# Folding mirrored rows before stage one of a Fourier mixing and maxout kernel

## The chip, the cores and the metric

The kernel runs on one core of a Trainium2 chip. A core has five engines with queues of their own: TensorE (PE in the profile; its weight loads are PEld) multiplies matrices, VectorE (DVE) and ScalarE (ACT) work on elements, GpSimd (POOL) copies, adds and starts indirect DMAs, and SyncE (SP) starts most DMAs. The metric is the device time of one execution in microseconds.

## The reference

For 8 batches of 3072 tokens by 256 features, the input goes through a Fourier transform over tokens and one over features; the real part is kept. Each of the 24576 tokens then goes through a maxout layer:

```python
X = np.fft.fft(x, axis=1); X = np.fft.fft(X, axis=2); y = X.real
h = np.maximum(np.maximum(y @ w1, y @ w2), y @ w3)      # 256 -> 768
out = h @ w_out                                         # 768 -> 256
```

The input is real. So the result of a feature pair d and 64 - d (in the kernel's layout of four groups of 64 features) can be got from a few real sums, and the token k and its mirror image 3072 - k share most of the work.

## The kernel before

**Stage one** (method `s` of `Mix`, pieces s0 to s6). Tokens are split as 24 x 128. A batch lies on 96 partitions, four groups of 24: partition (g, a) holds feature group g of token row a, with 128 tokens bb and 64 features dl along the free axis. TensorE takes, for a feature d of 33, the 96x128 rows as weights and a table of 96 columns as the moving operand. Each feature needs two matmuls into the same PSUM columns: one (L496) with the rows as they are and the table m24f, one (L498) with the *mirrored* rows (feature 64 - d of the mirrored token) and m24r. Pieces s0 to s5 do five features each; s6 does features 0 (52 columns), 32 (48) and 1 (96). The result z is evicted by ScalarE (L503).

**The rows for it** (`turn_chunk`, `reverse`). A batch is loaded in four chunks of 32 token columns, fp32, into a pool of four tiles xs (L107; the chunk's one extra row by L119). GpSimd casts each chunk to bf16 and to the order feature by token: two casts for the rows as they are (L155, `v[:, 0:33]`) and two for the mirrored ones (L158, `v[:, 33:66]`, read backwards within the partition). The bf16 tile x0 is in a pool of two. Batch 0 is loaded as bf16 and laid out by ScalarE and VectorE during the set-up.

**Stage two** (pieces k0 to k5, `end`). TensorE multiplies z with tables (L522, L524); ScalarE evicts to t, whose halves tE and tO are the even and odd parts of a batch (two buffers).

**The layer.** A batch is 18 *units*: 3 blocks of 512 columns by 6 chunks of 128 hidden features. `unit_plus` (L542, L543) makes two PSUM banks pse2 and pse3 from te and to; ScalarE takes the relu of the first (L556, tile stmp), VectorE the maximum with the second (L557, tile hp). `finish`, one unit later, subtracts through gD into the same banks (`unit_minus`, L550) and again makes relu and maximum (tile hm): that is the mirrored half of the tokens. pse2 and pse3 have two banks each, so `unit_plus` of a unit waits until hm of the unit but one before is read out. The second product (L567) is spread between the units as a queue of small steps (`l2_some`); per 128 tokens VectorE makes other (L594) and ot (L617), GpSimd adds even (L597) and scatters half of ot by an indirect DMA (L620), and SP stores the other half (L630). ot is in a pool of six.

**Order.** Every engine runs its queue in the order in which the program emits it. A table `plan` says which work is emitted behind which unit; `at(b, unit, fn)` counts units from the start of batch b and runs over into the next batch. While batch b is multiplied, the pieces of batch b + 1 are emitted one per unit from `begin[b]` on, the casts of batch b + 2 behind units 6 to 21, and the loads of batch b + 3 behind units 18, 19, 20 and 22 (that is 0, 1, 2 and 4 of the next batch; 6 after batch 0). SP's queue holds loads and stores together.

## Time and profile before

| | us |
|---|---|
| median of 3 runs | 413.23 |
| lowest, highest | 412.5, 413.6 |
| profiled execution | 412.64 |
| its span | 410.9 |
| VectorE, hp and hm (L557), 288 of | 0.69 each |
| VectorE, ot (L617) and other (L594), 92 of each | 0.68 and 0.48 each |
| GpSimd, casts (L155, L158) of 96x512 to 96x561 | 1.05 to 1.16 each |
| GpSimd, even (L597) and scatter (L620), 92 of each | 0.72 and 1.12 each |

How to read it: the profile gives each engine's busy time and its share of the span; a chain of waits, followed back from the last instruction; the queue of every engine as a timeline (start, duration, engine, line, output<-inputs, partitions x elements; in brackets the idle time before and what ended it); and waits by engine. Busy is not the same as bound: matmuls overlap, so a matmul's cost is the distance between starts. The 1.7 us between the span and the execution's time lie around the program.

### The profile page before, as it was taken

What the parts mean: (1) busy time and instruction counts of PE and PEld (TensorE: products, weight loads), DVE (VectorE), ACT (ScalarE), POOL (GpSimd) and SP (SyncE); (2) the same over time, 40 slices, a digit from 0 to 9 for tenths busy, and PEclk for the clock granted to TensorE, in tenths of its full rate; (3) what the DMA queues carried; (4) which work ended last, traced back from release to release, by engine and by line L of the source; (5) the groups of instructions that cost most, each with busy time, mean ns of one, the idle gap of its engine ahead of it and who ended that gap; (6) DMA issues with size and microseconds to landing.
All of it is one profiled execution on the core that took longest, in us unless ns stands there. A gap on an engine that the chain in (4) does not pass through costs nothing.

```text
span 410.9 us, 9097 instructions
## 1 busy us (share of the span) xinstructions
PE 397.4 (97%) x3072; PEld 269.2 (66%) x3072; DVE 308.7 (75%) x556; ACT 266.5 (65%) x489; POOL 320.7 (78%) x428
## 2 busy tenths in 40 slices
PE   0999999999999999999999999999999999999996
PEld 0465677766676677667666667667666666766665
DVE  8798767776768777786778777787768767778884
ACT  6787766766666667657765766666775676655550
POOL 9599999998888888888789798888878844446651
PEclk9999999999999999999999999999999999999999
DMA  9999885784228841586218942386411121212214
GB/s 116 185 198 183 188 210 143 184 193 104 100 80 210 181 130 53 144 209 139 99 65 191 193 133 86 95 195 144 143 65 70 61 78 64 79 53 53 104 65 142
DMA packets 131111, 52.70 MB, mean 128 GB/s; under 512 B 113009, under 2 KB 128120, under 8 KB 131064
## 3 DMA queue, kind: packets, MB, share of 16 engines
q1 hardware_dynamic: 106496, 37.50, 37.5%
q0 software_dynamic: 23632, 14.29, 16.3%
q8 instruction: 24, 0.39, 0.4%
q10 hardware_dynamic: 936, 0.33, 0.3%
q14 instruction: 23, 0.19, 0.2%
HBM read 29.02 MB, written 25.17 MB: 132 GB/s over the span
## 4 chain that ended last, share of the span: by engine, by line
PE 95%; DVE 2%; ACT 1%; issue 0%; POOL 0%; ACTq 0%; POOLq 0%
PE po L567 30%; PE pse L542 15%; PE pse L550 15%; PE pse L543 15%; PE ps L496 3%; PE ps L498 3%; PE po L591 3%; PE ps L522 3%; PE ps L524 3%; PE pl L580 2%; PE warm L713 2%; DVE hm L557 1%; PE psw L465 0%; DVE w L276 0%; ACT stmp L556 0%
## 5 line engine op out<-in xcount | busy, mean ns | idle before, releaser
L556 ACT ACTIVATE stmp<-pse 128x512 bf16<-128x512 f32 x288 | 171.2, 600 | 44.7 <-PE pse L543 29.7
L557 DVE TENSOR_TENSOR hp<-pse,stmp 128x512 bf16<-128x512 f32 x144 | 99.6, 691 | 87.2 <-ACT stmp L556 60.1
L620 POOL DMA_INDIRECT out_dram<-ot,rows_m x92 | 102.8, 1118 | 53.2 <-DVE ot L617 40.1
L542 PE MATMUL pse<-t,gE 128*128 128x512 bf16 x288 | 109.2, 379 | 0.5
L543 PE MATMUL pse<-t,gO 128*128 128x512 bf16 x288 | 109.0, 378 | 0.0
L557 DVE TENSOR_TENSOR hm<-pse,stmp 128x512 bf16<-128x512 f32 x144 | 99.2, 689 | 3.8 <-ACT stmp L556 3.5
L567 PE MATMUL po<-wout_bf,hp 128*128 128x256 bf16 x576 | 85.9, 272 | 0.0
L550 PE MATMUL pse<-t,gD 128*128 128x512 bf16 x288 | 85.6, 379 | 0.0
L567 PE MATMUL po<-wout_bf,hm 128*128 128x256 bf16 x570 | 85.3, 273 | 0.0
L597 POOL TENSOR_TENSOR even<-even,other 128x256 f32<-128x256 f32 x92 | 66.5, 723 | 22.3 <-DVE other L594 19.8
L567 PEld LDWEIGHTS <-hp 128*128 128x128 bf16 x576 | 56.3, 98 | 17.1 <-issue 1.9
L567 PEld LDWEIGHTS <-hm 128*128 128x128 bf16 x576 | 56.4, 98 | 16.6
L617 DVE TENSOR_TENSOR ot<-po,even 128x512 f32<-128x512 f32 x92 | 62.8, 682 | 0.0
L158 POOL CAST x<-xs 96x544 bf16<-96x544 f32 (+5 forms) x57 | 60.7, 1071 | 0.0
L155 POOL CAST x<-xs 96x544 bf16<-96x544 f32 (+2 forms) x51 | 59.0, 1159 | 0.3 <-DMA xs<-in_x_dram 0.3
L526 ACT CAST t<-ps 128x512 bf16<-128x512 f32 x48 | 27.9, 586 | 34.5 <-PE ps L524 34.4
L550 PEld LDWEIGHTS <-gD 128*128 128x128 bf16 x288 | 27.9, 98 | 32.2
L503 ACT CAST z_all<-ps 128x480 bf16<-128x480 f32 x46 | 25.4, 560 | 33.7 <-PE ps L498 33.7
L594 DVE SCALAR_TENSOR_TENSOR other<-twice,po 128x256 f32<-128x256 f32 x92 | 43.8, 476 | 0.1
L543 PEld LDWEIGHTS <-gO 128*128 128x128 bf16 x288 | 28.1, 98 | 20.3 <-issue 2.0
L542 PEld LDWEIGHTS <-gE 128*128 128x128 bf16 x288 | 28.1, 98 | 19.6 <-issue 0.7
L583 ACT COPY even<-pl 128x512 f32<-128x512 f32 x46 | 27.0, 588 | 10.1 <-PE pl L580 10.1
(171 smaller groups left out, 383.7 us busy)
## 6 DMA issues: line engine op xcount, KB each, us to landing
xs<-in_x_dram SPq DMA_DIRECT2D x84, 198.0 KB
out_dram<-ot SPq DMA_DIRECT2D x90, 128.0 KB
xs<-in_x_dram SPq DMA_DIRECT2D x28, 192.0 KB
raw_w<-in_moe_w_dram SPq DMA_DIRECT2D x4, 384.0 KB
out_dram<-ot,rows_m POOLq DMA_INDIRECT x92, 3.8
out_dram<-ot SPq DMA_DIRECT2D x17, 64.0 KB
x<-in_x_dram POOLq DMA_DIRECT2D x8, 120.0 KB, 6.1
xs<-in_x_dram SPq DMA_DIRECT2D x32, 5.8 KB
```

The lines of the kernel that those rows point to most:

```text
L155: nc.gpsimd.tensor_copy(v[:, d0:d1, ch * 32:ch * 32 + 32], xs[:, 0:32 * 64].rearrange("p (bb dl) -> p dl bb", dl=64)[:, d0:d1, :])
L158: reverse(lambda out, in_: nc.gpsimd.tensor_copy(out, in_), v[:, 33:66, :], xs, ch * 32, 33 if ch == 3 else 32, 32 + d0, 32 + d1)
L542: nc.tensor.matmul(pse[:, 0:n], gE[i][:, js], te, start=True, stop=False)
L543: nc.tensor.matmul(pse[:, 0:n], gO[i][:, js], to, start=False, stop=True)
L550: nc.tensor.matmul(pse, gD[i][:, js], to, start=False, stop=True, skip_group_check=True)
L556: nc.scalar.activation(out=stmp[:, 0:n], in_=pses[0][:, 0:n], func=AX.Relu)
L557: nc.vector.tensor_tensor(out=dst, in0=src3, in1=stmp[:, 0:n], op=ALU.max)
L567: nc.tensor.matmul(po, hcols(jc), wout_bf[:, jc * 256:(jc + 1) * 256], start=False, stop=(jc == NJC - 1), skip_group_check=True)
L594: nc.vector.scalar_tensor_tensor(out=other, in0=twice, scalar=po[:, 256:257], in1=po[:, 0:256], op0=ALU.mult, op1=ALU.subtract)
L597: nc.gpsimd.tensor_tensor(out=line[:, 256:512], in0=line[:, 0:256], in1=other, op=ALU.add)
L617: nc.vector.tensor_tensor(out=ot, in0=po, in1=lin, op=ALU.add)
L620: stored(nc.gpsimd.indirect_dma_start(out, bass.IndirectOffsetOnAxis(ap=rows_m[0:128 - lo, b * 12 + slot: b * 12 + slot + 1], axis=0), ot[ ...
```

## The change

For batches 2 to 7 the two halves are added before TensorE sees them. GpSimd writes only the mirrored half, bf16, into one tile xb (`mirror_chunk`, eight copies of 96x512, and four small ones for feature 0). Eight DMAs (`send_turned`) write xb to DRAM with the order of the partitions turned, one DMA (`fetch_turned`) reads it back into the tile xp, so that mirrored rows lie on the partitions of the rows they belong to. VectorE adds each raw fp32 chunk and xp into xw, bf16 (`fold_chunk`, eight adds). Stage one then takes one matmul per feature with xw, except feature 0, which keeps two. xb, xp and xw are one tile each. The casts of the plain half on GpSimd are gone, and a raw chunk is now held until its adds are done, so that the loads of batch b + 3 are emitted behind the adds. Stage-one pieces begin one to three units later, s6 first; x0, now used by batches 0 and 1 alone, has one buffer.

```diff
--- before.py
+++ after.py
@@ -60,7 +60,8 @@
     consts = ctx.enter_context(tc.tile_pool(name="consts", bufs=1))
     ps_f = ctx.enter_context(tc.tile_pool(name="ps_f", bufs=2, space=bass.MemoryType.PSUM))
     xs_pool = ctx.enter_context(tc.tile_pool(name="xs", bufs=4))
-    x0_pool = ctx.enter_context(tc.tile_pool(name="x0", bufs=2))
+    x0_pool = ctx.enter_context(tc.tile_pool(name="x0", bufs=1))
+    turn_pool = ctx.enter_context(tc.tile_pool(name="turn", bufs=2, space=bass.MemoryType.DRAM))
     t_pool = ctx.enter_context(tc.tile_pool(name="tbuf", bufs=2))
 
     m24f = consts.tile([96, 96], BF16, tag="m24f")
@@ -95,6 +96,11 @@
     t_mid = consts.tile([128, 2, B], BF16, tag="t_mid")
     z_all = consts.tile([128, 128 * 26], BF16, tag="z_all")
     z = z_all.rearrange("p (c r) -> p c r", r=26)
+    xb = consts.tile([96, 33 * 128], BF16, tag="xb")
+    mir = xb.rearrange("p (dl bb) -> p dl bb", bb=128)
+    xp = consts.tile([96, 33 * 128], BF16, tag="xp")
+    xw = consts.tile([96, 34 * 128], BF16, tag="xw")
+    xwv = xw[:, 0:33 * 128].rearrange("p (dl bb) -> p dl bb", bb=128)
 
     def x_rows(b):
         return x[b].rearrange("(a bb) (g dl) -> g a bb dl", bb=128, g=4)
@@ -141,22 +147,58 @@
                      in_=bass.AP(xs.tensor, xs.offset + (m - 1) * 64 + lo,
                                  [xs.ap[0], [1, hi - lo], [-64, m]]))
 
-    def turn_chunk(b, ch, part=None):
+    def turn_chunk(b, ch):
 
         if (b, "v") not in turned:
-            x0 = x0_pool.tile([96, 66 * 130], BF16, name="x0", tag="x0")
-            v = x0.rearrange("p (dl bb) -> p dl bb", bb=130)
+            x0 = x0_pool.tile([96, 68 * 128 + 32], BF16, name="x0", tag="x0")
+            v = x0[:, 0:66 * 130].rearrange("p (dl bb) -> p dl bb", bb=130)
             turned[b] = (lambda d: v[:, d, 0:128], rows_back(v[:, 33:66, :]))
             turned[b, "v"] = v
         v = turned[b, "v"]
         xs = raw[b, ch]
-        for (d0, d1) in (((0, 17), (17, 33))[part % 2:part % 2 + 1] if part is not None else ((0, 33),)):
-            if part is None or part < 2:
-                nc.gpsimd.tensor_copy(v[:, d0:d1, ch * 32:ch * 32 + 32],
-                                      xs[:, 0:32 * 64].rearrange("p (bb dl) -> p dl bb", dl=64)[:, d0:d1, :])
-            if part is None or part >= 2:
-                reverse(lambda out, in_: nc.gpsimd.tensor_copy(out, in_), v[:, 33:66, :], xs,
-                        ch * 32, 33 if ch == 3 else 32, 32 + d0, 32 + d1)
+        nc.gpsimd.tensor_copy(v[:, 0:33, ch * 32:ch * 32 + 32],
+                              xs[:, 0:32 * 64].rearrange("p (bb dl) -> p dl bb", dl=64)[:, 0:33, :])
+        reverse(lambda out, in_: nc.gpsimd.tensor_copy(out, in_), v[:, 33:66, :], xs,
+                ch * 32, 33 if ch == 3 else 32)
+
+    def mirror_chunk(b, ch, part):
+
+        xs = raw[b, ch]
+        c0 = 96 - 32 * ch
+        d0, d1 = ((0, 16), (16, 32))[part]
+        nc.gpsimd.tensor_copy(mir[:, d0:d1, c0:c0 + 32],
+                              bass.AP(xs.tensor, xs.offset + 32 * 64 + 32 + d0,
+                                      [xs.ap[0], [1, d1 - d0], [-64, 32]]))
+        if part:
+            nc.gpsimd.tensor_copy(mir[:, 32, c0:c0 + 32],
+                                  bass.AP(xs.tensor, xs.offset + 32 * 64, [xs.ap[0], [-64, 32]]))
+
+    held = {}
+
+    def send_turned(b):
+
+        hd = turn_pool.tile([8, 12 * 4096], BF16, name="held", tag="held")
+        for i in range(8):
+            nc.sync.dma_start(out=hd[7 - i].rearrange("(a r) -> a r", a=12),
+                              in_=xb[i * 12:(i + 1) * 12, 0:4096])
+        held[b] = hd
+
+    def fetch_turned(b):
+
+        hd = held[b]
+        nc.sync.dma_start(out=xp[:, 0:4096],
+                          in_=bass.AP(hd.tensor, hd.offset + 11 * 4096,
+                                      [[12 * 4096, 8], [-4096, 12], [1, 4096]]))
+
+    def fold_chunk(b, ch, part, eng=nc.vector):
+
+        d0, d1 = ((0, 17), (17, 33))[part]
+        xs = raw[b, ch]
+        eng.tensor_tensor(
+            out=xwv[:, d0:d1, ch * 32:ch * 32 + 32],
+            in0=xs[:, 0:32 * 64].rearrange("p (bb dl) -> p dl bb", dl=64)[:, d0:d1, :],
+            in1=bass.AP(xp.tensor, xp.offset + (32 - d0) * 128 + ch * 32,
+                        [xp.ap[0], [-128, d1 - d0], [1, 32]]), op=ALU.add)
 
     def signed():
         nc.scalar.activation(out=gw[:, 514:770], in_=gw[:, 256:512], func=AX.Copy, scale=sgn)
@@ -199,8 +241,8 @@
         nc.gpsimd.iota(t, pattern, base=base, channel_multiplier=cm,
                        allow_small_or_imprecise_dtypes=True)
 
-    x0_first = x0_pool.tile([96, 64 * 130], BF16, name="x0", tag="x0")
-    x0v = x0_first.rearrange("p (bb dl) -> p bb dl", dl=64)
+    x0_first = x0_pool.tile([96, 68 * 128 + 32], BF16, name="x0", tag="x0")
+    x0v = x0_first[:, 0:64 * 128].rearrange("p (bb dl) -> p bb dl", dl=64)
     xs_a = xs_pool.tile([96, 33 * 64], FP32, name="xs", tag="xs")
     rows_a = xs_a.rearrange("p (bb dl) -> p bb dl", dl=64)
     load_rows((nc.sync, nc.sync, nc.scalar, nc.scalar), rows_a[:, 0:16, :], 0, 112, 128)
@@ -412,6 +454,7 @@
     first_op = nc.gpsimd.memset(mark, 0.0)
     tc.add_manual_dep(first_op.ins, laid.ins.name, AFTER, reason="the two share a port")
     nc.gpsimd.memset(two_row, 0.0)
+    nc.gpsimd.memset(xp[:, 4096:4224], 0.0)
     nc.gpsimd.memset(two_row[0:1], 2.0)
     nc.gpsimd.memset(gw[:, 512:513], 0.0)
     nc.gpsimd.memset(gw[0:1, 512:513], 1.0)
@@ -493,10 +536,15 @@
                 parts = [(0, 52, m0f, m0r), (32, 48, m24f, m24r), (1, 96, m24f, m24r)]
             c0 = 0
             for (d, n, mf, mr) in parts:
-                nc.tensor.matmul(ps1[:, c0:c0 + n], x0[0](d), mf[:, 0:n],
-                                 start=True, stop=False)
-                nc.tensor.matmul(ps1[:, c0:c0 + n], x0[1](d), mr[:, 0:n],
-                                 start=False, stop=True)
+                if x0 is not None:
+                    pairs = ((x0[0](d), mf), (x0[1](d), mr))
+                elif d:
+                    pairs = ((xwv[:, d, :], mf),)
+                else:
+                    pairs = ((xwv[:, 0, :], mf), (mir[:, 32, :], mr))
+                for i, (st, mv) in enumerate(pairs):
+                    nc.tensor.matmul(ps1[:, c0:c0 + n], st, mv[:, 0:n], start=(i == 0),
+                                     stop=(i == len(pairs) - 1))
                 c0 += n
             if k < len(DLS):
                 lo = 4 * DLS[k][0]
@@ -766,7 +814,7 @@
     def piece(b, what):
         mm = mix(b)
         if what[0] == "s":
-            mm.s(int(what[1:]), turned[b])
+            mm.s(int(what[1:]), turned.get(b))
         elif what[0] == "k":
             mm.k(int(what[1]))
         else:
@@ -777,8 +825,9 @@
 
     ahead = (("s0",), ("s1",), ("s2",), ("s3",), ("s4",), ("s5",), ("s6",),
              ("k0",), ("k1",), ("k2",), ("k3",), ("k4",), ("k5", "end"))
+    order_of = (6, 0, 1, 2, 3, 4, 5)
     first_ahead = (11, 12, 13, 13, 14, 14, 15, 16, 16, 17, 18, 19, 20)
-    begin = [11, 6] + [5] * (B - 3)
+    begin = [11, 9, 8, 7] + [6] * (B - 5)
 
     def l2_first():
         for _ in l2_even(0, 0):
@@ -801,15 +850,26 @@
         at(0, (6, 7, 9, 11)[ch], lambda ch=ch: fetch(2, ch))
     for b in range(B - 1):
         for i, whats in enumerate(ahead):
+            if b and i < 7:
+                whats = (f"s{order_of[i]}",)
             for what in whats:
-                at(b, begin[b] + i if b else first_ahead[i], lambda b=b, what=what: piece(b + 1, what))
+                at(b, min(begin[b] + i, 17 if b == B - 2 else 99) if b else first_ahead[i],
+                   lambda b=b, what=what: piece(b + 1, what))
         if b + 2 < B:
-            for ch in range(4):
-                for part in range(4):
-                    at(b, 6 + 4 * ch + part if b else 11 + 11 * (4 * ch + part) // 16,
-                       lambda b=b, ch=ch, part=part: turn_chunk(b + 2, ch, part))
-                if b + 3 < B:
-                    at(b, UNITS + (0, 1, 2, 4 if b else 6)[ch], lambda b=b, ch=ch: fetch(b + 3, ch))
+            mirror_at, send_at, fold_at = (
+                ((11, 12, 13, 13, 14, 15, 16, 17), 18, 23),
+                ((10, 11, 12, 12, 13, 14, 15, 16), 17, 22),
+                ((9, 10, 11, 12, 13, 13, 14, 15), 16, 21),
+                ((8, 9, 10, 11, 12, 12, 13, 14), 15, 20))[min(b, 3)]
+            for i in range(8):
+                at(b, mirror_at[i], lambda b=b, i=i: mirror_chunk(b + 2, i // 2, i % 2))
+            at(b, send_at, lambda b=b: send_turned(b + 2))
+            at(b, send_at + 2, lambda b=b: fetch_turned(b + 2))
+            for i in range(8):
+                at(b, fold_at + i // 2, lambda b=b, i=i: fold_chunk(b + 2, i // 2, i % 2))
+            if b + 3 < B:
+                for ch in range(4):
+                    at(b, fold_at + 1 + ch, lambda b=b, ch=ch: fetch(b + 3, ch))
 
     for b in range(B):
         mm = mixes[b]
```

## The prediction

> **What bounds the kernel now.** I read the page first: busy time of each engine (part 1) and the chain that ended last (part 4).
>
> ```profile
> PE 397.4 (97%) x3072; PEld 269.2 (66%) x3072; DVE 308.7 (75%) x556; ACT 266.5 (65%) x489; POOL 320.7 (78%) x428
> PE 95%; DVE 2%; ACT 1%; issue 0%; POOL 0%; ACTq 0%; POOLq 0%
> ```
>
> TensorE is busy 97% of the span and makes up 95% of the chain. Asked for its waits, the trace names one only, 9.6 us at the start. So a matmul taken away from the steady part shortens the run by its own interval, and each wait that TensorE gains lengthens it in full. Next I read the timeline of TensorE where stage one runs (a piece of batch 4, while batch 3 is multiplied):
>
> ```profile
> 181.18 0.21 PE L496 MATMUL ps<-m24f,x 96*128 96x96 bf16 x1
> 181.22 0.20 PE L498 MATMUL ps<-m24r,x 96*128 96x96 bf16 x1
> 181.27 0.20 PE L496 MATMUL ps<-m24f,x 96*128 96x96 bf16 x1
> ...
> 181.60 0.38 PE L542 MATMUL pse<-t,gE 128*128 128x512 bf16 x1
> ```
>
> The durations overlap; what counts is start to start. Ten matmuls take 181.18 to 181.60, so 0.042 us each. Last I read VectorE in the units where the change will put its adds (batch 5, units 2 to 5), and TensorE beside it:
>
> ```profile
> 269.02 0.47 DVE L594 SCALAR_TENSOR_TENSOR other<-twice,po 128x256 f32<-128x256 f32 x1
> 269.41 0.68 DVE L617 TENSOR_TENSOR ot<-po,even 128x512 f32<-128x512 f32 x1
> 270.04 0.69 DVE L557 TENSOR_TENSOR hp<-pse,stmp 128x512 bf16<-128x512 f32 x1
> 270.69 0.69 DVE L557 TENSOR_TENSOR hm<-pse,stmp 128x512 bf16<-128x512 f32 x1
> 271.30 0.47 DVE L594 SCALAR_TENSOR_TENSOR other<-twice,po 128x256 f32<-128x256 f32 x1
> 272.50 0.69 DVE L557 TENSOR_TENSOR hp<-pse,stmp 128x512 bf16<-128x512 f32 x1 [0.73 <-PE pse L550]
> ...
> 274.78 0.69 DVE L557 TENSOR_TENSOR hp<-pse,stmp 128x512 bf16<-128x512 f32 x1 [0.34 <-PE pse L550]
> ...
> 277.51 0.69 DVE L557 TENSOR_TENSOR hp<-pse,stmp 128x512 bf16<-128x512 f32 x1 [0.40 <-ACT stmp L556]
> ```
>
> ```profile
> 271.24 0.38 PE L542 MATMUL pse<-t,gE 128*128 128x512 bf16 x1
> 271.67 0.38 PE L542 MATMUL pse<-t,gE 128*128 128x512 bf16 x1
> ```
>
> The number in brackets is VectorE's idle time before the instruction. A unit without stage-one or stage-two work lasts about 2.3 us on TensorE. In the four units VectorE is idle for 0, 0.73, 0.34 and 0.40 us, 1.47 us in all. And TensorE follows closely: the unit's matmuls into the second bank (271.67) need the bank that hm releases; that hm runs from 270.69 to 271.38, 0.29 us earlier. With two pse3 banks, TensorE can be ahead of VectorE by no more than that 0.29 us. This is where the change is decided.
>
> **The change, part by part**
>
> *Matmuls removed.* For each of batches 2 to 7, the six full pieces lose 5 each, 30 x 0.042 = 1.26 us; piece 6 loses one of 96 columns (0.040, by a last piece at 150.53 to 150.57) and one of 48 (0.025). Together 1.33 us a batch, 8.0 us over six. Weight loads go with them. All of it lies on the chain: minus 8.0 us.
>
> *VectorE adds.* Eight a batch (two per unit in four units), four of 96x544 and four of 96x512, fp32 rows plus bf16 rows out to bf16. The nearest rows: two-operand TENSOR_TENSOR from SBUF at L271, 128x512 in 0.685 us; L190, fp32 and bf16 to bf16, 128x768 in 0.95 us; and for the strided read, the CAST at L140, 96x544 in 0.643 us. That makes 0.69 to 0.72 us each. VectorE starts the next instruction about 0.08 us before the end of the one in front (hp 270.04, hm 270.69), so an add moves the queue by 0.64 (544) or 0.61 us (512): 1.25 us a unit. The units' own work stays.
>
> I put them into the timeline above, each start being the one before plus its interval. Unit 2: adds at 270.04 and 270.68, hp at 271.29, hm 271.93 to 272.62; TensorE's second bank at 272.68 instead of 271.67, 1.0 us late. Unit 3: other 272.54, adds 272.94 and 273.58, hp 274.19, hm 274.83 to 275.52; bank at 275.58 instead of 273.94 (unit 4 lasts 2.28 us), 1.6 late. Unit 4: ot 275.44, adds 276.06 and 276.70, hp 277.31, hm 277.95 to 278.64; 2.4 late. Unit 5: other 278.56, ot 278.96, adds 279.58 and 280.22, hp 280.83, hm 281.47 to 282.16; 3.4 late. Then VectorE is idle again and TensorE leads. Check by sums: 4 x 1.25 = 5.0 us of adds less 1.47 idle and 0.29 of lead leave 3.2. I take 3.4 us a batch, 20.4 us over six: plus 20.4. Ends: with intervals of 0.55 us (the CAST's duration less the overlap) 8 x 0.55 - 1.76 = 2.6, 16 us in all; with whole durations that don't overlap 8 x 0.70 - 1.76 = 3.9, 23 us.
>
> The first three batches have their adds in units 5 to 8, 4 to 7 and 3 to 6; stage one and two are moved behind (begin 9, 8, 7, 6), so these too are bare units, and I take the same price. Piece 6, first in the new order, needs the last add; that ends at 280.9, TensorE reaches the piece at about 280.6, and the wait falls inside the 3.4.
>
> *GpSimd.* Sixteen casts a batch (1.05 to 1.16 us) become eight of 96x512 (1.075 us by the row of that shape) and four of 96x32 (0.23). No wait of TensorE is on GpSimd now, so the relief is worth nothing. The clear of xp's last 128 columns joins a queue of GpSimd's setup at 19 us; a like one (L414) takes 0.20 us; 0 to 0.2 us, I take 0.
>
> *DMAs.* A batch gains eight DMAs of 96 KB out and one of 768 KB in, all on SP. A store's issue there takes 0.33 us, so the eight about 2.6 us. At the 242 GB/s that the loads reached (170 to 172 us, DMA share 0.96) 0.79 MB takes 3.2 us. The send stands behind unit 15, the fetch two units later, the first add behind unit 20: with three units of 2.7 and two of 2.3 us the whole trip has 12.7 us. Transfer time alone as each hop: 2.6 + 3.2 + 3.2 = 9.0 us, 3.7 to spare. Landing times of the start (4.9 us for 192 KB, 6.6 for 96 KB) as each hop: 2.6 + 6.6 + 6.6 = 15.8, 3.1 late. Those were taken at full DMA load; in the send's units the DMA share was 0.03 to 0.42, so I am nearer the first and take 0. If late, VectorE stands at the first add and TensorE with it, so it costs in full, up to 18.6 us over six. Behind the fetch on SP stand stores; they only hold ot, of which there are six, and one is used every 3.9 us.
>
> *Loads of x.* They start behind the adds, units 3 to 6 instead of 0 to 4, and take some 24 us (168.4 to 192.1 in SP's timeline, batch 3), so the last chunk lands in about unit 13, where its mirror copy stands. GpSimd may wait there by a unit; the other two outputs of its queue (even, the scatter) have a bank each of slack. I take 0, up to 1 us a batch.
>
> *Fewer x0 buffers.* Batch 1's tile waits for readers of the first, done by 20 us; its first copy starts at 30.4 us. Nothing.
>
> Sum against the profiled execution (412.64 us, span 410.9): 412.64 - 8.0 + 20.4 = 425.0. The median of the runs, 413.23, is 0.6 higher: 425.6 us.
>
> [...] Two adds like these already ran beside GpSimd: L190 on VectorE from 20.79 for 0.95 us, while GpSimd cast from 20.77 to 21.87, and from 22.23 for 1.05 us, while GpSimd worked from 21.95 to 23.14. By the line through L271 one takes 0.96 us, so VectorE lost at most 0.1 us. [...]
>
> **Rivals**
>
> 1. The adds run faster than one element a cycle. For: L295, 128x896 bf16 in 0.42 us. Against: L271 and L190, both with two operands, do not. Below 0.39 us of interval ((1.33 + 1.47 + 0.29) / 8) the change gains; at 0.30 us it costs 0.64 us a batch, and the time is 413.2 - 8.0 + 3.8 = 409.0.
> 2. The adds wait for GpSimd. The trace has even start about 0.16 us after other ends, for 0.72 us. In two of the four units ot stands between, and the add would come 1.02 us after other's start, even ending at 1.35: 0.33 us each, 4 us in all: 429.6. Were the scatter's 1.0 us behind ot to hold the second add as well (0.57 us, three units of four), 10 us more: 440.
> 3. The mirrored rows come late. At half the bound, 1.5 us a batch: 434.6.
>
> **How the numbers follow.** Forecast 0.50 (422 to 428); GpSimd rival 0.18 (428 to 440); late transfer 0.15 (428 to 444); the adds partly absorbed in a way I do not see, 414 to 420, 0.07; within 0.3% (about what a measurement of this kernel can tell from no change) 0.02; faster adds 0.08. So faster 0.08, same 0.02, slower 0.90. The range 419 to 437 leaves out some 0.14 below and 0.06 above. The price of the adds moves the forecast by 4 us down or 3 up.
>
> **What would show it.** TensorE matmuls fall by 192. VectorE's new group has 48 adds of about 0.7 us. Waits of TensorE on hm or on VectorE appear, about 3.4 us in each of six windows of four units, each unit there lasting about 3.1 us; stage-one pieces last 0.21 us. If adds wait for a DMA, rival 3 holds; if they are much longer than 0.72 us or wait for even, rival 2. Wrong I would be if VectorE has idle time in those units that other instructions can give up, or if the adds are shorter than their rows.

## The result, and the profile after

The change made the kernel slower. The median is 450.74 us (449.97 to 453.64, four runs) against 413.42 us (412.5 to 413.7) before: a ratio of 1.092, 95% interval 1.087 to 1.097. The direction was forecast; the size was not. The forecast was 425.6 us with a range of 419 to 437, so 25.1 us are missing.

The line numbers of the changed kernel: the add is L197, the mirrored copies are L169 and L173, the sends L182, the fetch L189, stage one L546, `unit_plus` L590 and L591, `unit_minus` L598, hp and hm L605, other L642, ot L665, even L645.

Busy time and chain, from the page of the kernel after:

```profile
PE 401.9 (89%) x2880; PEld 263.5 (59%) x2880; DVE 356.4 (79%) x604; ACT 266.4 (59%) x489; POOL 281.4 (63%) x399
PE 55%; DMA 13%; DVE 13%; SPq 7%; issue 6%; POOL 3%; ACT 2%; DVEq 0%; ACTq 0%; POOLq 0%
```

The 192 matmuls are gone (3072 to 2880) and VectorE has 48 instructions more. But TensorE, 97% busy before, is at 89% of a longer span, and the chain that was 95% TensorE now passes through VectorE, the DMAs and SP's queue. What TensorE and VectorE wait for (in all, times, longest):

```profile
PE pse L590 <- DVE hm L605: 29.5, 22, 3.7
...
DVE xw L197 <- DMA xp<-held: 7.3, 5, 2.6
```

The first line did not exist before. It is the forecast's mechanism: TensorE stands in `unit_plus` until VectorE, which now has the adds in its queue, has read out hm. The forecast gave it 20.4 us; it is 29.5. The second is the rival of the late transfer: VectorE, and TensorE behind it, stand at the first add of five batches. VectorE's timeline in one fold window:

```profile
242.47 2.02 DVE L197 TENSOR_TENSOR xw<-xs,xp 96x544 bf16<-96x544 f32 x2 [0.94 <-DMA xp<-held]
244.40 0.68 DVE L605 TENSOR_TENSOR hp<-pse,stmp 128x512 bf16<-128x512 f32 x1
245.00 0.68 DVE L605 TENSOR_TENSOR hm<-pse,stmp 128x512 bf16<-128x512 f32 x1
245.59 0.48 DVE L642 SCALAR_TENSOR_TENSOR other<-twice,po 128x256 f32<-128x256 f32 x1
245.99 2.45 DVE L197 TENSOR_TENSOR xw<-xs,xp 96x544 bf16<-96x544 f32 x2
248.37 0.67 DVE L605 TENSOR_TENSOR hp<-pse,stmp 128x512 bf16<-128x512 f32 x1
248.96 0.67 DVE L605 TENSOR_TENSOR hm<-pse,stmp 128x512 bf16<-128x512 f32 x1
249.56 0.67 DVE L665 TENSOR_TENSOR ot<-po,even 128x512 f32<-128x512 f32 x1
250.16 2.01 DVE L197 TENSOR_TENSOR xw<-xs,xp 96x544 bf16<-96x544 f32 x2
```

A pair of adds moves the queue by 1.93 us (242.47 to 244.40), not by 1.25 as forecast, and the second pair by 2.38. GpSimd's even runs from 246.16 for 1.44 us beside that second pair, where it takes 0.73 us alone. TensorE in the same window:

```profile
242.88 0.38 PE L591 MATMUL pse<-t,gO 128*128 128x512 bf16 x1
245.73 0.38 PE L590 MATMUL pse<-t,gE 128*128 128x512 bf16 x1 [2.48 <-DVE hm L605]
...
248.53 0.63 PE L590 MATMUL pse<-t,gE 128*128 128x512 bf16 x1
248.96 0.63 PE L591 MATMUL pse<-t,gO 128*128 128x512 bf16 x1
```

After the pause of 2.48 us the matmuls start 0.43 us apart instead of 0.22 for a while (248.53 to 248.96): the clock granted to TensorE is 0.82 from 244 to 248 us and 0.75 from 248 to 252 us, 1.00 before. So a pause of this length can cost more than itself. It does not always: after the start the trace has five pauses of over 2 us, and the mean granted clock of the 4 us behind them is 0.65 (after 2.18 us), 0.60 (3.61), 0.60 (2.48), 1.00 (2.39) and 0.50 (3.70).

### The profile page after: what moved, and what is told of

It is laid out like the page before. It is cut to its first block, busy times and chain, and to the rows that moved or that the text cites. A ratio compares the mean times of both kernels' runs of the same rounds, so it can differ in the third digit from the quotient of the medians.

```text
span 449.6 us, 8805 instructions
## 1 busy us (share of the span) xinstructions
PE 401.9 (89%) x2880; PEld 263.5 (59%) x2880; DVE 356.4 (79%) x604; ACT 266.4 (59%) x489; POOL 281.4 (63%) x399
## 4 chain that ended last, share of the span: by engine, by line
PE 55%; DMA 13%; DVE 13%; SPq 7%; issue 6%; POOL 3%; ACT 2%; DVEq 0%; ACTq 0%; POOLq 0%
PE po L615 17%; PE pse L590 9%; PE pse L598 9%; PE pse L591 8%; DMA xp<-held 7%; DMA held<-xb 4%; DVE hm L605 4%; SPq L182 4%; DVE hp L605 3%; DVE xw L197 3%; PE ps L546 3%; SPq L113 2%; PE warm L761 2%; PE pl L628 2%; PE po L639 1%
## 5 line engine op out<-in xcount | busy, mean ns | idle before, releaser
L668 POOL DMA_INDIRECT out_dram<-ot,rows_m x92 | 108.4, 1179 | 88.7 <-DVE ot L665 76.5
L605 DVE TENSOR_TENSOR hp<-pse,stmp 128x512 bf16<-128x512 f32 x144 | 99.1, 688 | 70.9 <-ACT stmp L604 55.0
L590 PE MATMUL pse<-t,gE 128*128 128x512 bf16 x288 | 111.1, 386 | 30.2 <-DVE hm L605 29.5
L591 PE MATMUL pse<-t,gO 128*128 128x512 bf16 x288 | 110.6, 384 | 0.0
L645 POOL TENSOR_TENSOR even<-even,other 128x256 f32<-128x256 f32 x92 | 70.7, 769 | 63.5 <-DVE other L642 60.9
L605 DVE TENSOR_TENSOR hm<-pse,stmp 128x512 bf16<-128x512 f32 x144 | 98.7, 685 | 4.1 <-ACT stmp L604 2.4
L615 PE MATMUL po<-wout_bf,hp 128*128 128x256 bf16 x576 | 87.5, 276 | 0.0
L615 PE MATMUL po<-wout_bf,hm 128*128 128x256 bf16 x570 | 86.6, 276 | 0.0
L598 PE MATMUL pse<-t,gD 128*128 128x512 bf16 x288 | 86.5, 382 | 0.0
L665 DVE TENSOR_TENSOR ot<-po,even 128x512 f32<-128x512 f32 x92 | 62.7, 681 | 0.0
L591 PEld LDWEIGHTS <-gO 128*128 128x128 bf16 x288 | 28.4, 99 | 54.5 <-issue 38.9
L197 DVE TENSOR_TENSOR xw<-xs,xp 96x544 bf16<-96x544 f32 (+1 forms) x48 | 51.7, 1115 | 7.5 <-DMA xp<-held 7.3
L169 POOL CAST xb<-xs 96x512 bf16<-96x512 f32 x48 | 51.1, 1072 | 0.3 <-DMA out_dram<-ot 0.2
L598 PEld LDWEIGHTS <-gD 128*128 128x128 bf16 x288 | 28.3, 98 | 33.4 <-issue 2.1
L642 DVE SCALAR_TENSOR_TENSOR other<-twice,po 128x256 f32<-128x256 f32 x92 | 43.7, 475 | 0.1
L590 PEld LDWEIGHTS <-gE 128*128 128x128 bf16 x288 | 28.6, 99 | 20.5 <-issue 1.8
```

Of the source, the lines that this page charges most:

```text
L169: nc.gpsimd.tensor_copy(mir[:, d0:d1, c0:c0 + 32], bass.AP(xs.tensor, xs.offset + 32 * 64 + 32 + d0, [xs.ap[0], [1, d1 - d0], [-64, 32]]))
L197: eng.tensor_tensor(out=xwv[:, d0:d1, ch * 32:ch * 32 + 32], in0=xs[:, 0:32 * 64].rearrange("p (bb dl) -> p dl bb", dl=64)[:, d0:d1, :], i ...
L590: nc.tensor.matmul(pse[:, 0:n], gE[i][:, js], te, start=True, stop=False)
L591: nc.tensor.matmul(pse[:, 0:n], gO[i][:, js], to, start=False, stop=True)
L598: nc.tensor.matmul(pse, gD[i][:, js], to, start=False, stop=True, skip_group_check=True)
L605: nc.vector.tensor_tensor(out=dst, in0=src3, in1=stmp[:, 0:n], op=ALU.max)
```

## The experiments

**e1, the adds alone.** A kernel that runs VectorE and GpSimd instructions in groups of six, first VectorE alone with one property of the add changed at a time, then both engines together.

```diff
+    add(V, i, rows(xs, 0, 17), back(xp, 0, 17), cols_(i, 0, 17))     # as in the kernel
...
+    add(V, i, dense(xs, 0, 17), back(xp, 0, 17), cols_(i, 0, 17))    # raw rows dense
...
+    V.tensor_copy(out=cols_(i, 0, 17), in_=rows(xs, 0, 17))          # one input
...
+    stage(lambda i: add(V, i, rows(xs, 0, 17), back(xp, 0, 17), cols_(i, 0, 17)), even)   # beside GpSimd
```

> A kernel of VectorE and GpSimd instructions alone, no reference output; each form of add is repeated six times. In the changed kernel an add (96x544 and 96x512) took 0.99 to 1.48 us, median 1.07, where the prediction had 0.69 to 0.72. Theory 1 (the form of the operands costs it): with GpSimd silent the add as in the kernel still takes about 1.0 us, and one of the forms with rows or mirrored rows read densely takes 0.72 us or less. Theory 2 (GpSimd beside it costs it): alone the add takes 0.72 us, and 1.0 us or more only beside GpSimd's adds or copies. For the pairs of 2.4 us instead of 2.0 in the changed kernel both theories expect an add beside GpSimd's even to be longer by up to 0.5 us; if neither is, something else made them long.

VectorE's timeline of this kernel: two adds as in the kernel; two with dense raw rows; six casts with one strided input; then, beside GpSimd, six adds with even, six with mirrored copies, six dense adds with even, six casts with even.

```profile
17.82 1.90 DVE L94 TENSOR_TENSOR w<-xs,xp 96x544 bf16<-96x544 f32 x2
28.99 1.36 DVE L94 TENSOR_TENSOR w<-xs,xp 96x544 bf16<-96x544 f32 x2
60.31 3.33 DVE L113 CAST w<-xs 96x544 bf16<-96x544 f32 x6
106.19 8.38 DVE L94 TENSOR_TENSOR w<-xs,xp 96x544 bf16<-96x544 f32 x6
115.00 10.47 DVE L94 TENSOR_TENSOR w<-xs,xp 96x544 bf16<-96x544 f32 x6
125.89 6.97 DVE L94 TENSOR_TENSOR w<-xs,xp 96x544 bf16<-96x544 f32 x6
133.29 6.21 DVE L152 CAST w<-xs 96x544 bf16<-96x544 f32 x6
```

GpSimd's timeline: six times even alone, and beside the first group of adds.

```profile
84.74 4.73 POOL L134 TENSOR_TENSOR ga<-ga,gb 128x256 f32<-128x256 f32 x6
106.04 7.68 POOL L134 TENSOR_TENSOR ga<-ga,gb 128x256 f32<-128x256 f32 x6
```

Per add and start to start, once a group runs: 0.97 us in the kernel's form, 0.64 us with dense raw rows or with everything dense. The other variants say which property it is. Mirrored rows read upwards 0.97, mirrored rows in fp32 0.97, raw rows in bf16 0.98, a step of 65 instead of 64 elements 1.03: none of these matters much. One is far worse: with the features innermost, so that the raw rows are consecutive and the mirrored rows and the output have the step, an add takes 2.42. A cast that reads the same strided rows as its only input takes 0.54 us. So a row with the strided read alone (0.54) and one with the second input alone (0.64) both lie far below a row with both (0.97). The step is not free for the cast either: a dense cast of 96x2112 earlier in this kernel takes 1.26 us, 0.60 ns an element, and the strided one 0.99 ns. So a step of 256 bytes costs both, the add 0.33 us (0.64 to 0.97) and the cast by its time per element; what makes it cost that, no run shows.

Beside GpSimd the two engines take turns. Three instructions from the middle of the first group:

```profile
111.02 1.31 POOL L134 TENSOR_TENSOR ga<-ga,gb 128x256 f32<-128x256 f32 x1
111.72 1.47 DVE L94 TENSOR_TENSOR w<-xs,xp 96x544 bf16<-96x544 f32 x1
112.41 1.31 POOL L134 TENSOR_TENSOR ga<-ga,gb 128x256 f32<-128x256 f32 x1
```

The add starts in the middle of an even and ends 0.85 us after it; the next even starts in the middle of that add and ends 0.54 us after it. So most of the time that each takes alone lies behind the end of the other, and both engines have the same period: 1.39 us for an add and an even (alone 0.97 and 0.80), 1.75 for an add and a mirrored copy (0.97 and 1.09), 1.16 for a dense add and an even (0.64 and 0.80), 1.03 for a cast with one input and an even (0.54 and 0.80). Both engines lose. The two rows of the set-up by which the prediction put VectorE's loss at 0.1 us or less were too few, beside other GpSimd instructions. The cast with its single input loses as well (1.03 us against 0.54).

**e2, no adds; e3, no transfers; e4, dense rows.** Each takes one thing from the changed kernel. In e2 xw is cleared once and in e3 xp, so that e2 leaves out the rows and e3 their mirrored half; e4 reads as many raw elements without a step, which leaves out the order of the rows.

```diff
-            for i in range(8):                                            # e2
-                at(b, fold_at + i // 2, lambda b=b, i=i: fold_chunk(b + 2, i // 2, i % 2))
...
-            at(b, send_at, lambda b=b: send_turned(b + 2))                # e3
-            at(b, send_at + 2, lambda b=b: fetch_turned(b + 2))
...
-            in0=xs[:, 0:32 * 64].rearrange("p (bb dl) -> p dl bb", dl=64)[:, d0:d1, :],
+            in0=xs[:, d0 * 32:d1 * 32].rearrange("p (dl bb) -> p dl bb", bb=32),   # e4
```

> VectorE's adds are left out (xw is cleared once and holds zeros), everything else of the change stays: mirror copies, both transfers, later loads, one matmul per feature. If VectorE's adds are the whole loss, this takes 413.4 - 8.0 = 405.4 us, 404 to 407. If the transfers on SP's queue, the later loads or the later pieces cost by themselves, it is above 408.

> Both transfers are left out (xp is cleared once, so the adds add zeros), all else of the change stays. VectorE waited 7.3 us for xp in the profile of the changed kernel. If that wait is on the path in full, 450.7 - 7.3 = 443.4 us or a little less; if it lies in time that is lost anyway, 448 to 451.

> The add reads its fp32 input from consecutive elements instead of with a step of 64 elements (256 bytes); wrong rows, so the output is not the reference's; all else of the change stays. If the step is what doubles the add, adds take 0.7 us and the time falls to 425 to 433 us (the prediction's 425.6 and up to 7 us for late transfers). If it is not the step, 448 to 453 us.

e2: 415.24 us, ratio 1.007 (1.004 to 1.010): 35.5 us below the changed kernel, but not below the kernel before, although 8 us of matmuls are gone. Its waits:

```profile
POOL xb L169 <- DMA xs<-in_x_dram: 19.2, 9, 5.0
DVE ot L665 <- POOL even L645: 13.4, 12, 2.8
...
PE po L639 <- DVE ot L665: 6.0, 6, 2.0
```

The loads, now emitted later, hold GpSimd's mirrored copies; even stands behind these, ot behind even, TensorE behind ot. The forecast had put this at 0, up to 1 us a batch. (e8 below shows that the transfers have a part in it.)

e3: 444.95 us, 1.079 (1.075 to 1.083). The transfers cost 5.8 us. Without them the granted clock is 1.000 over the whole span (0.981 with them) and no wait of TensorE on VectorE is longer than 1.8 us: the loss of clock belongs to the long pauses that the transfers make, and is part of the 5.8.

e4: 442.95 us, 1.072 (1.068 to 1.077). A pair of adds takes 1.31 us where no even is beside it, but the gain is 7.8 us only, since VectorE comes to its first add earlier and waits there: for xp 13.9 us instead of 7.3.

**e5, dense rows and no transfers.** The two edits of e3 and e4 together: the case that the prediction had worked out unit by unit.

> The add reads consecutive fp32 elements and both transfers are left out (xp holds zeros). Adds then cost 0.65 us each, the price that the prediction used, and nothing waits for xp. If the prediction's working unit by unit was right apart from the price of the add and the late transfer, this takes 425 to 429 us. If it is 432 us or more, a third cost is left (the later loads, adds that meet GpSimd, or TensorE's clock).

429.23 us, 1.040 (1.037 to 1.042). The forecast's sum for cheap adds that wait for nothing was 425.6. So its queue of VectorE, its leads and its idle times hold within 3.6 us. The rest fits the meetings with even and not the loads, for which GpSimd waits 1.3 us here. A pair of adds moves the queue by 1.23 us where no even is near (7 pairs; the forecast had 1.25), by 1.46 where its first add starts inside an even (10), and by 1.77 where an even starts beside it (7): 6.0 us more in all. That is close to what the prediction's second rival gave in its smaller form, 429.6: it had two meetings a batch at 0.33 us, the trace has 0.22 and 0.54.

**e6, no adds and the loads as early as before.** To see whether the loads explain e2.

```diff
-                    at(b, fold_at + 1 + ch, lambda b=b, ch=ch: fetch(b + 3, ch))
+                    at(b, UNITS + (0, 1, 2, 4 if b else 6)[ch], lambda b=b, ch=ch: fetch(b + 3, ch))
```

> As the run without adds, but the loads of the batch after next are emitted where the kernel before has them (units 18, 19, 20 and 22 or 24) instead of behind the places of the adds. If GpSimd's waits for late rows (19.2 us on xs in the run without adds) and what follows from them (even, then ot, then TensorE) are what kept that run at 415 us, this takes 404 to 407 us. If the two transfers or the later pieces hold it, 412 to 416 us.

425.39 us, 1.030 (1.027 to 1.033): 10 us worse than e2. The waits that grew:

```profile
DVE ot L665 <- DMA out_dram<-ot: 16.4, 7, 4.9
PE po L639 <- DVE ot L665: 13.3, 5, 4.3
```

In SP's queue four loads stand right behind the fetch and take up to 9.8 us to issue (182.78 us), and the stores of ot stand behind them; so the buffers of ot, which the forecast thought ample, run out. That the loads come late is what one sees in e2; that they could simply be put back fell with this run.

**e8, neither adds nor transfers.** e2 with the edit of e3.

> VectorE's adds and both transfers are left out (xw holds zeros); mirror copies, the later loads and one matmul per feature stay. If the two transfers are what kept the run without adds at 415 us (they fill SP's queue, behind which loads and stores stand), this takes 404 to 407 us, the prediction's gain of 8.0 us in full. If the loads being later by themselves keep it, 411 to 415 us.

409.21 us, 0.992 (0.989 to 0.994). Of the 8.0 us of matmuls 3.6 appear. The transfers are worth 6.0 us here, as in e3. In its profile (of an execution of 411.96 us) GpSimd still waits 10.6 us for the loads, ot 7.8 us for even and TensorE 3.8 us for ot. The 4.4 us that are still missing fit that chain, though no run isolates the loads. Without any add the change as laid out could not have reached its full gain.

**e7, the adds in bf16.** GpSimd casts the plain rows again, straight into xw, and VectorE adds xp onto xw in place, dense and in bf16, one stage-one piece at a time. The mirrored copies, the sends and the loads have other units.

```diff
+        nc.gpsimd.tensor_copy(xwv[:, d0:d1, ch * 32:ch * 32 + 32],
+                              xs[:, 0:32 * 64].rearrange("p (bb dl) -> p dl bb", dl=64)[:, d0:d1, :])
...
+    def fold_rows(d0, d1):
+        nc.vector.tensor_tensor(
+            out=xw[:, d0 * 128:d1 * 128].rearrange("p (dl bb) -> p dl bb", bb=128),
+            in0=xw[:, d0 * 128:d1 * 128].rearrange("p (dl bb) -> p dl bb", bb=128),
+            in1=bass.AP(xp.tensor, xp.offset + (32 - d0) * 128,
+                        [xp.ap[0], [-128, d1 - d0], [1, 128]]), op=ALU.add)
...
+                at(b, UNITS + begin[b + 1] + i - 1, lambda i=i: fold_piece(order_of[i]))
```

> All computed. GpSimd casts the plain rows too, as in the kernel before (mirror copies first), so raw chunks come free and are loaded where the kernel before loads them; VectorE adds bf16 to bf16 with consecutive tokens, in the seven pieces that stage one takes, one a unit, the unit ahead of its matmuls; the transfer has a longer lead. If the form of the operands and the late loads are the two causes, an add of 96x640 takes 0.4 us or less, and the time is 405 to 409 us, below the kernel before. If two SBUF inputs as such are slow (0.75 us for 640), adds make TensorE late by 0.1 to 0.4 us in each of seven units of six batches: 412 to 425 us.

434.57 us, 1.054 (1.050 to 1.058). An add of 96x640 takes 0.48 us where GpSimd is quiet, and up to 2.67 us where GpSimd casts; once an add waited 10.2 us for xp.

**e9, e10, e11: the casts kept away from the adds, in two, eight and sixteen blocks of the transfer.** As e7, with GpSimd's sixteen casts in units 13 to 23, the adds behind them, and the loads in units 21 to 24; e9 sends and fetches two blocks of 48 rows, e10 the change's eight blocks of 12, e11 sixteen of 6.

```diff
-            nc.sync.dma_start(out=hd[7 - i].rearrange("(a r) -> a r", a=12),
-                              in_=xb[i * 12:(i + 1) * 12, 0:4096])
+            nc.sync.dma_start(out=hd[1 - i].rearrange("(a r) -> a r", a=48),       # e9; e11: 6
+                              in_=xb[i * 48:(i + 1) * 48, 0:4096])
...
-                                      [[12 * 4096, 8], [-4096, 12], [1, 4096]]))
+                                      [[48 * 4096, 2], [-4096, 48], [1, 4096]]))   # e11: 16, 6
```

> All computed. As the run with bf16 adds, but GpSimd's sixteen casts lie in the eleven units without adds, so that adds meet only even and the scatter; the mirrored rows are sent by two DMAs of 48 partitions instead of eight of 12, and the loads are emitted behind the fetch. If adds that meet GpSimd's casts and a late fetch are what made that run 434.6 us, adds of 96x640 take 0.48 us with few above 1 us, and the time is 405 to 413 us. If it is the amount of DMA work or GpSimd's queue, 418 us or more.

> All computed. The run with adds apart had its 768 KB fetch described as 2 blocks of 48 rows; while nothing else ran, 2 of the 16 DMA engines were busy (share 0.12), and VectorE waited up to 13.3 us. Here rows are sent in 8 blocks of 12 and fetched so, as in the change; all else as in that run. If the number of blocks is the number of DMA engines that the fetch gets, it lands 6 us or so after its issue instead of 20, VectorE's wait for it falls from 74.9 us to under 15, adds of 96x640 take 0.48 us with few above 1 us, and the time is 408 to 418 us. If the fetch is slow for another reason, 450 us or more.

> As the run with 8 blocks, with 16 blocks of 6 rows. By the same theory the fetch gets all 16 engines and lands some 3 us sooner than with 8, and waits for it vanish; sixteen sends of about 0.5 us each lie on SP's queue instead of eight, 4 us more a batch. 406 to 416 us; not slower than with 8 blocks unless SP's queue becomes the limit.

e9: 489.91 us, 1.189 (1.184 to 1.194). TensorE is idle from about 92.5 us on, while the fetch that SP began at 82.32 us is under way. Stretches of it (length, PE busy, then the other engines, granted clock, DMA share, GB/s):

```profile
95.00:100.00 5.00, 0.00 (x0) 0.00 (x0) 0.00 (x0) 0.00 (x0) 0.00 (x0) 0.72 0.12 49
100.00:104.00 4.00, 0.00 (x0) 0.00 (x0) 0.08 (x1) 0.00 (x0) 0.00 (x0) 0.50 0.32 82
```

A DMA share of 0.12 is 1.9 of sixteen engines, about as many as the fetch has blocks (two); that the blocks set the number was the author's inference, and no run shows it by itself. The first add of that batch came at 103.92, 21.6 us after the fetch's issue, and the clock had meanwhile gone to 0.50.

e10: 443.43 us, 1.075 (1.072 to 1.079). The median add takes 0.48 us and the longest 1.13 now, but VectorE waits 24.6 us for xp, 5.1 at most. e11: 446.73 us, 1.082 (1.079 to 1.084), with 39.6 us of waits for xp in its profile (of its slowest execution, 451.19 us). The fetch itself is shorter (6.1 to 8.1 us from its issue to the add that waits for it, instead of 8.7 to 9.7), but sixteen sends keep SP's queue 7.5 to 9.9 us instead of 4.1 to 4.9, so it begins later.

**e12, the same with more lead.** As e10, with stage one and the adds one unit later, the fetch one unit earlier, and the loads emitted after the stores (units 23 to 26).

```diff
-    begin = [11] + [7] * (B - 2)
+    begin = [11] + [8] * (B - 2)
...
-            at(b, send_at + 2, lambda b=b: fetch_turned(b + 2))
+            at(b, send_at + 1, lambda b=b: fetch_turned(b + 2))
```

> All computed. As the run with 8 blocks and adds apart, with a longer lead for the transfer: the fetch is emitted one unit behind the sends instead of two, the loads two units later so that they don't run beside it, stage one and its adds one unit later. In the run before VectorE waited 24.6 us for xp. If that wait, and TensorE's lower clock after it (0.968 on average), is all that keeps it above the kernel before, the wait falls under 5 us and the time is 404 to 412 us. If the wait goes and the time stays above 420 us, something else holds it.

425.38 us, 1.030 (1.025 to 1.035): 18 us gained, and only 0.6 us of waits for xp are left. The earlier place of the fetch has little part in it: it begins 7.0 to 7.6 us after the first send, in e10 7.2 to 8.0, since in both SP waits for the sends to land. The later adds and the loads that no longer run beside the fetch were not tried apart. TensorE now waits at stage one:

```profile
PE ps L558 <- DVE xw L202: 10.1, 5, 2.1
```

The first piece needed features 0, 1 and 32, so both halves of GpSimd's plain casts, the last of which was still running.

**e13, with the pieces in the order in which the casts are done.** Plain casts of features 0 to 16 first, for all chunks; the piece with 0, 1 and 32 is third.

```diff
-    order_of = (6, 0, 1, 2, 3, 4, 5)
+    order_of = (0, 1, 6, 2, 3, 4, 5)
...
-                at(b, lay_at[i], lambda b=b, i=i: lay_chunk(b + 2, i // 2, i % 2))
+                at(b, lay_at[i], lambda b=b, i=i: lay_chunk(b + 2, i % 4, i // 4))
```

> All computed. As the run with a longer lead, but feature piece 6, which needs the last plain rows, is third in the order instead of first, and GpSimd casts the plain rows of the low features of all chunks first. In the run before TensorE stood five times about 2.0 us and 0.5 us behind it, waiting for VectorE's add of feature 32, which waited for GpSimd's last plain cast, and its clock was lower for some us after each. If this wait is all that is left of the loss, TensorE has no wait over 1 us in the steady part and the time is 405 to 411 us, below the kernel before. If one add a unit still costs TensorE something by itself, 412 us or more without a wait for GpSimd.

414.83 us, 1.006 (1.003 to 1.009); granted clock 1.000. TensorE's waits after the start:

```profile
PE po L651 <- DVE ot L677: 5.6, 5, 1.1
PE pse L602 <- DVE hm L617: 0.9, 5, 0.2
```

The adds and the transfers no longer stop TensorE. What is left is GpSimd, which holds all sixteen casts: five times even comes 1.1 us late, and ot with it.

**e14, e15: GpSimd's casts spread over more units.** Only the units change.

```diff
-  mirror_at, lay_at = ((13, 13, 14, 15, 15, 16, 17, 17), (18, 18, 19, 20, 20, 21, 22, 23))
+  mirror_at, lay_at = ((11, 12, 13, 14, 14, 15, 16, 17), (12, 15, 17, 18, 19, 20, 21, 22))   # e14
+  mirror_at, lay_at = ((11, 12, 13, 14, 14, 15, 16, 17), (13, 15, 16, 18, 18, 19, 20, 21))   # e15
```

> The whole transform is computed. Nothing is taken away from the run before; only the units at which GpSimd makes its casts are changed, for batches 3 to 7: mirrored copies behind units 11 to 17 instead of 13 to 17, plain casts behind 12, 15, 17 to 22 instead of 18 to 23. In the run before, GpSimd stood 1.0 to 1.8 us idle four times in units 9 to 12, and then worked without a break until unit 23, where even came 1.1 us late and TensorE waited 1.10 to 1.13 us for ot five times (5.6 us). Theory (those five waits are all that keeps the run from the full gain of the matmuls): they go, and the time is 414.8 - 5.6 = 409.2, 408 to 411, under the kernel before's 413. Rival (GpSimd has no room at all; its backlog only moves): ot waits for even elsewhere, 413 to 417. Second rival: the first plain cast, now behind unit 12, waits for TensorE's reads of the rows of the batch before, and holds even there: 412 to 418.

> The whole transform is computed. As the run beside it, with the plain casts behind units 13, 15, 16, 18, 18, 19, 20, 21: one unit earlier in most places, so that the last cast lies before the scatter that takes 2.57 us in unit 22 or 23. Theory (the five waits come from the casts that lie behind that long scatter): no wait for ot is left, 408 to 410, at or below the run beside it. Rival (the backlog is what counts, not the place): casts are packed closer in units 15 to 18, ot waits there, 410 to 416.

423.99 us (1.022, 1.016 to 1.027) and 419.04 us (1.014, 1.011 to 1.017): both theories and both rivals were wrong about the place. The waits for ot are gone, but casts now stand beside the last adds of the batch before. VectorE's and GpSimd's timelines in e14:

```profile
203.72 3.54 DVE L202 TENSOR_TENSOR xw<-xw,xp 96x640 bf16<-96x640 bf16 x1
```

```profile
203.12 1.07 POOL L169 CAST xb<-xs 96x512 bf16<-96x512 f32 x1
204.16 0.71 POOL L657 TENSOR_TENSOR even<-even,other 128x256 f32<-128x256 f32 x1
204.83 1.10 POOL L197 CAST xw<-xs 96x544 bf16<-96x544 f32 x1
205.88 1.03 POOL L169 CAST xb<-xs 96x512 bf16<-96x512 f32 x1
206.87 0.48 POOL L173 CAST xb<-xs 96x32 bf16<-96x32 f32 x1
```

One add of 0.48 us lasts 3.54 us, from 203.72 to 207.26: as long as GpSimd goes from one cast to the next, and it ends inside the small last one. GpSimd's casts have their usual length (1.03 to 1.10); only the small one is longer than its 0.23. So here VectorE lets four GpSimd instructions pass before its turn, where the adds of e1 had one after each. The traces differ in one more thing: in e1 each GpSimd instruction starts 0.06 to 0.08 us after the end of the one before, here 0.03 to 0.05 us before it. Whether that decides it is not shown. TensorE, waiting for that piece's rows, stood 1.79 us. In e15 four adds last 2.5 us in the same way, and VectorE also waits 7.3 us for xp.

**e16, e17: one or two casts of a batch on ScalarE.** e13 again, with the last (e16) or the last two (e17) plain casts of each batch made by ScalarE.

```diff
-                at(b, lay_at[i], lambda b=b, i=i: lay_chunk(b + 2, i % 4, i // 4))
+                at(b, lay_at[i], lambda b=b, i=i: lay_chunk(b + 2, i % 4, i // 4,
+                                  nc.scalar.copy if i == 7 else None))   # e17: i > 5
```

> The whole transform is computed. As the lead-in-order run of 414.83 us, but the last plain cast of each of batches 2 to 7 (96x512, 1.07 us, behind unit 23) is made by ScalarE instead of GpSimd; ScalarE has idle time of 0.8 and 2.2 us in those units. No cast is moved towards the adds. Theory (the matmuls' 8.0 us come back once GpSimd is no longer behind): the five waits of 1.10 to 1.13 us for ot (behind even) fall to about 0.1 us, and the time is 414.8 - 5.0 = 409.8, 408.5 to 411. Rival (ScalarE's relu comes late instead: hp waits for stmp 36 us already): TensorE waits for hp or hm, 412 to 416.

> The whole transform is computed. As the run beside it, with the last two plain casts of a batch on ScalarE. Theory: the waits were 1.1 us, so one cast is enough and the second gains at most 0.1 us a wait: 408 to 410.5. Rival (ScalarE is late by the second cast): 411 to 416.

e16: 408.69 us, 0.991 (0.989 to 0.993), 0.9% below the kernel before and the best of the study. TensorE's waits after the start:

```profile
PE pse L602 <- DVE hm L617: 1.2, 6, 0.2
PE po L651 <- DVE ot L677: 0.7, 4, 0.2
PE ps L582 <- ACT t L586: 0.2, 1, 0.2
```

The five waits of 1.1 us are gone, and 4.2 of the 8.0 us are there; these waits are 2.1 us more of it, and where the last 1.7 us are was not found. e17: 412.41 us, 0.999 (0.998 to 1.001). The time is in the rival's range, and its waits are there: its casts on ScalarE take 1.29 us in the mean (1.07 in e16), hm comes later (1.7 us) and stmp too (1.0 us). These waits in its profile add up to 1.7 us more than in e16, while the medians differ by 3.7; the rest isn't explained.

## Why the prediction was right or wrong

Taken in one order, the runs divide the 25.1 us between forecast and result so: from 425.6 to 429.2 (e5) the meetings with even, 3.6; from 429.2 to 445.0 (e3) the form of the add, 15.7; from 445.0 to 450.7 the transfers, 5.8. Through e4 instead of e3 the transfers cost 13.7 and the form 7.8: the shorter the adds, the longer VectorE waits for the rows. An account that doesn't hang on the order is the prediction's own check by sums. Its 413.2 - 8.0, less 1.76 us of idle time and lead in each of six batches, leaves 394.6; to this come the distances by which the 48 adds move VectorE's queue and the waits for xp, now read from each trace (an estimate, in us):

| | 48 adds | waits for xp | sum | measured |
|---|---|---|---|---|
| forecast's values | 30.0 | 0 | 424.6 | |
| changed kernel | 49.9 | 7.3 | 451.8 | 450.74 |
| e3, no transfers | 51.1 | 0 | 445.7 | 444.95 |
| e4, dense rows | 34.1 | 13.9 | 442.6 | 442.95 |
| e5, both | 35.6 | 0 | 430.2 | 429.23 |

The sum meets all four runs within 1.1 us. So the mechanism of the forecast was right, and two of its terms were mis-sized: the adds (30.0 instead of 49.9) and the wait for the rows (0 instead of 7.3).

- *Matmuls removed, minus 8.0.* 192 are gone. What they are worth could not be seen in the changed kernel; the best run shows 4.2 of them (408.69 against 412.89) while TensorE still waits 2.1 us for other engines. The sums above use all 8.0 and come out, which is no test of its own.
- *VectorE adds, plus 20.4.* This is the step that failed. The place and the mechanism were right (waits on hm in the fold windows), the size was not: the interval taken was 0.64 and 0.61 us, and it is 0.97 us with nothing beside it and 0.97 to 1.19 in the kernel (half a pair). The two rows behind it each had one property of the add, a second SBUF input (L271, L190) or a strided read (L140), and the larger was taken. The bounds were made from the same rows, 0.55 to 0.70, so they missed too. e5, with the form changed to one that does take 0.64 us, gave back the forecast within 3.6 us: the timeline was sound, its price was not. (In the forecast's upper end 8 x 0.70 - 1.76 is 3.8, not 3.9; the 23 us stand.)
- *GpSimd, 0; rival 2.* Put at nothing on two rows of the set-up, and wrong: an add that meets even waits for its turn, and so does even. In the changed kernel the 12 pairs of adds without even move the queue by 1.93 us, the six whose first add starts inside an even by 2.07, the six beside which one starts by 2.37. That is 3.5 us over six batches (6.0 in e5), near the rival's smaller figure of 4. Its larger one is refuted: pairs beside the scatter alone last 2.00 to 2.04 us, like those with nothing beside them.
- *DMAs, 0; rival 3.* The mirrored rows were late in five batches, up to 2.6 us; 5.8 us in all by e3 with the loss of clock, which the forecast did not have. It named the right bound (15.8 us for the trip, 3.1 late) and took the wrong end, because the DMA share in the send's units was low. From the first send to the first add the trip took 13.7 to 15.6 us, and 12.7 were at hand. The chain of the changed kernel that leads to the fold window above (in the order of time: start, duration, what):

```profile
228.37 0.18 POOL xb L173
228.56 0.17 SPq L182
...
232.13 3.75 DMA held<-xb
...
235.95 6.34 DMA xp<-held
```

Issuing the sends takes 4.1 to 4.8 us (forecast 2.6), the last one lands 3.75 us after its issue begins, and the fetch, which has to wait for that, takes 6.34 (forecast 3.2 each).
- *Loads of x, 0 to 1 a batch.* Without adds they cost: in e8 GpSimd waits 10.6 us for them and 4.4 us of the gain are missing. The bank of slack was argued for each output alone, while a late cast stops all that stands behind it on GpSimd. With adds no such loss shows: in e5 GpSimd waits 1.3 us for them.
- *Rival 1 (faster adds).* False for this form (0.97 us for 544 elements, 1.78 ns each). Dense bf16 rows, which e16 uses, are faster: 0.48 us for 640, 0.75 ns each. How long a cycle of VectorE is, the unit of the rival's bound, no run shows.

## What to carry to other kernels

Price an instruction by a row that has all its properties together: two rows with one property each (0.54 us strided, 0.64 us with two inputs) gave no bound for both (0.97 us). Where VectorE adds two SBUF tensors, look at what GpSimd does in those units before counting its duration (here 0.97 us alone, a period of 1.39 beside even), and move the GpSimd work rather than the add. When a trip through DRAM is put beside a busy queue, count the issue time and the landing of every hop, and leave lead for the whole trip: one unit more of it, and loads that no longer run beside the fetch, were worth 18 us here.

## What the runs showed that was not expected

- VectorE and GpSimd took turns, instruction by instruction: an fp32 add and an even had a common period of 1.39 us, against 0.97 and 0.80 alone. But a dense bf16 add of 0.48 us beside a row of GpSimd instructions without gaps waited for four of them and lasted 3.54 us, while the casts kept their length. What decides whose turn it is stays open.
- TensorE's granted clock fell after four of the five pauses of 2.2 to 3.7 us in the changed kernel (to means of 0.50 to 0.65 over the next 4 us, and not after the one of 2.39 us), and in a pause of e9 to 0.72 (95 to 100 us) and 0.50 (100 to 104 us). In e3, where no pause is longer than 1.8 us, it stayed at 1.000; in e14, after five pauses of 1.8 us, it fell once (between 0.8 and 0.9 in the slice of its page from 157.6 to 168.1 us).
- The same scatter on GpSimd that takes 1.0 us took 2.56 us once a batch in e13 (232.90 us), while SP was issuing loads; its cause is open.
